# Clustered attention and two MLPs on one core: the order of the attention rewritten as one pipeline over a pair of heads

## The chip, the cores and the metric

One Trainium2 chip, one core of it. The metric is the device time of one execution in microseconds, the median over several runs. The engines are called as the profile calls them: PE (TensorE; PEld is its weight loads), DVE (VectorE), ACT (ScalarE), POOL (GpSimd) and SP (SyncE), whose only work here is to issue DMAs.

## What is computed

Two batches of eight heads, 768 tokens, 64 values a head, everything in 32-bit floats. Each query and key is assigned to the nearest of 16 centroids of its head; a query attends only to the keys of its own cluster. The 1536 rows of 512 values that come out go through two MLPs.

```
q_assign = argmax(q_n . c_n), k_assign = argmax(k_n . c_n)      # 16 clusters a head
scores = scale * q @ k.T, -1e9 where q_assign != k_assign
attn = exp(scores - max(scores)); attn = attn / (sum(attn) + 1e-9)
x = attn @ v                                                     # 1536 x 512
h = max(x @ w1, x @ w2, x @ w3); x = h @ w_out                   # 512 -> 768 -> 512
h = x @ w_in; h = max(0.01 * h, h); out = h @ w_out2             # 512 -> 2048 -> 512
```

## The kernel before

The kernel runs under a manual schedule: each engine executes its instructions in the order in which the program issues them, and waits by semaphores where it needs another engine's result. So the order in which the program is written decides what waits for what.

**Attention.** The 16 heads are 8 pairs. A pair has six units: a unit is one head and 256 of its 768 queries, in two halves of 128. Unit n goes through these steps, named by letters in the table ORDER:

- S0, S1 (`scores`, L608): the scores of a half, four matmuls into one of two score tiles in PSUM (`s`). Two matmuls read the operands q1 and k1, two read q2 and k2, which also hold the one-hot clusters and the mask.
- M0, M1 (`maxima`, L614): the row maximum, on DVE, out of PSUM.
- X0, X1 (`exps`, L620): the exponential, on ACT, from the score tile into one of six buffers `ee` in SBUF, with the row sum.
- R (`inverse`, L628, L629): the reciprocal of the sums, on DVE. Q0, Q1 (`normal`, L634): the division, on POOL.
- T0, T2, T4 (`transposes`, L641): four PE transposes each, into one of three PSUM tiles `t`. E0, E2, E4 (`out_of_psum`, L654 on ACT, L656 on DVE): the copy to `et`; WAYS says which engine, A or D.
- V (`values`, L664): 24 matmuls for two units at once, reading `rv`, into the one tile `o`. Y (`store`, L670): the copy of it on ACT into `acc`.

Beside these run, once a pair, the steps that prepare later pairs. G, C, H, Na, Nb, W, FA, FB find the clusters (PE, ACT, PE, DVE, DVE, POOL, DVE, DVE). O and P turn them into rows `oo`. QH, KH, QL, KL split q and k into high and low parts `qh`, `kh`, `ql`, `kl`. LD and LV load q, k and v of a pair (`rq`, `rk`, `rv`; three buffers of `rv`). D0 and D1 (`operands`, L537) are ten DMAs each on SP's queue, which put these parts together: D0 fills q1, k1 and the upper part of q2 from qh, kh, ql; D1 fills k2 from kl and, from `oo`, the mask rows of q2 and k2, first for the first head of the pair, then for the second.

ORDER has six rows, one for each unit of a pair. An entry `S0/-2` means step S0 of unit n+2 in row n, so scores run two units ahead of the transposes (`T0/0`), and the values of a pair of units end one unit behind (`V/1`). An entry `LV+2` means the load for two pairs later. BEGIN writes out the first three units by hand; ONCE inserts single steps, among them the fetches `f` and the pieces `w` that split the first MLP unit's weights (DVE and ACT); END is the seam to the MLPs.

**MLPs.** Matmuls 128x128 by 128x512 in three products for each block (`three`, L238 to L240), 3 blocks of 512 tokens, weight units 0 to 13. Weights come as raw words and are split on DVE and ACT while PE works (`Weights`).

Of the kernel before, what the change touches and what calls it, by code (L numbers as in the profile page):

```python
# [36 lines left out]
ORDER = (  # L37
# [6 lines left out]
)  # L44

BEGIN = (
# [4 lines left out]
)  # L51
# [3 lines left out]
ONCE = {  # L55
# [10 lines left out]
}  # L66
WAYS = ("ADA", "DAD")
ENGINE = {"QH": "A", "QH@1": "P", "KH": "P", "KL": "P", "KL@0": "D", "W": "P", "W@1": "D"}
WARM = (8, 4)
PACE = 0.16  # L70
FIRST = ("G", "C", "H", "Na", "Nb", "O", "P", "W", "FA", "FB", "QH", "KH", "QL", "LD", "LV")
SPARE = {"O": (2, 0), "O0": (2, 0), "O1": (3, 0)}
HALF = S // 2
# [7 lines left out]
def clustered_attention_mlps(  # L81
# [229 lines left out]
    with ExitStack() as att:  # L311
# [11 lines left out]
        until_transposes = att.enter_context(ExitStack())  # L323
        ep = pool(until_transposes, "ep", 6, side="right")
        until_exps = att.enter_context(ExitStack())
# [185 lines left out]

        def all_onehot_T(p, spare):
            oh = st[p]["oh"][:, D:].rearrange("p (t x) -> p t x", t=NQ // 2)
            ps = spare.bitcast(BF16)[:, 0:HALF]
            for t in range(NQ // 2):
                nc.tensor.transpose(ps[:, t * P : (t + 1) * P], oh[:, t, :], idb)

        def all_penalties(p, spare):
            oo = sm.tile([P, HALF], F32R, tag="oo", name=f"oo{p}", bufs=1)
            st[p]["oo"] = oo  # L520
            nc.scalar.activation(
                oo, spare.bitcast(BF16)[:, 0:HALF], AF.Identity, scale=gain2, bias=base2
            )
# [9 lines left out]
        def operands(p, part, heads=(0, 1), queue=nc.sync):  # L533
# [5 lines left out]
            for j in heads:  # L539
# [12 lines left out]
                else:  # L552
                    q1, q2, k1, k2 = s[j]
                    if part != 2:
                        dma(k2[0:D], s["kl"][r])
                    if part != 1 and p >= 2:
                        for b in range(4):
                            rows = slice((2 * b + j) * C, (2 * b + j + 1) * C)
                            cols = slice(b % 2 * HALF, (b % 2 + 1) * HALF)
                            dma((q2, k2)[b // 2][D : D + C, cols], s["oo"][rows])  # L560
                    elif part != 1:
                        dma(q2[D : D + C], s["oo"][j * C : (j + 1) * C])
                        dma(k2[D : D + C], s["oo"][(2 + j) * C : (3 + j) * C])
# [32 lines left out]
        def scores(n, i, parts=(0, 1)):  # L596
            p, j, g = unit(n)
            q1, q2, k1, k2 = st[p][j]
            if n not in un:
                un[n] = {"e": [], "sum": sums[n % len(sums)]}  # L600
            c0 = g * G + i * P
            if 0 in parts:
                un[n]["s", i], un[n]["spare", i] = bank()
            ps = un[n]["s", i]
            for part in parts:
                a, b, start = ((q1, k1, True), (q2, k2, False))[part]
                for lo, hi in ((0, 512), (512, S)):
                    nc.tensor.matmul(  # L608
                        ps[:, lo:hi], a[:, c0 : c0 + P], b[:, lo:hi], start=start, stop=not start
                    )  # L610
# [36 lines left out]
        def out_of_psum(n, k):  # L647
            p, j, g = unit(n)
            u = un[n]
            if k == 0:  # L650
                u["et"] = done[p, g, j] = etp.tile([P, NQ, G], F32, tag=f"et{j}", name=f"et{n}")
# [29 lines left out]

        def spare(p, op, ahead):

            if p < ahead:
                return scrap((op, p) if p == 0 else p)[:, 256 * p * int(op[1]) :]
            r, i = SPARE[op]
            return un[(p - ahead) * 2 * NG + r]["spare", i]

        def take_apart(op):

            u, c = int(op[1]), int(op[2])
            if op[0] == "f":
                weights.fetch(u, c)
                return
            if (u, c) not in pieces:
                pieces[u, c] = weights.piece(weights.raw.pop((u, c)), u, wa, c)
            next(pieces[u, c], None)

        def do(op, at):
# [25 lines left out]
            elif op == "O":  # L725
                all_onehot_T(at, spare(at, op, 1))
            elif op == "P":
                all_penalties(at, spare(at, "O", 1))
            elif o == "G":
                sims(at, d, spare(at, op, 2))  # L730
            elif op[0] == "N":
                j = int(op[1])
                if op[2] == "a":
                    near_max(at, j, spare(at, f"G{j}", 2))
                else:
                    near_eq(at, j)
            elif op == "W":
# [3 lines left out]
            elif op == "FB":  # L741
                first_eq(at)
            elif o == "O":
                onehot_T(at, d, spare(at, op, 1))
            elif o == "P":
                penalties(at, d, spare(at, f"O{d}", 1))
            elif o == "D":
# [23 lines left out]

        pieces, scraps = {}, {}
        if True:
# [57 lines left out]
            def start(op):  # L831
# [7 lines left out]
                elif op in ("LDq", "LDk"):  # L839
                    load_pair(1, op[2], nc.scalar)  # L840
                elif op in ("LV0", "LV1"):
                    load_pair(int(op[2]), "v", (nc.scalar, nc.sync)[int(op[2])])
                elif op in ("Wq", "Wk"):
# [22 lines left out]
                elif op == "in":  # L866
                    until_scores.close()
                    open_inputs()
                elif op == "ph":
                    until_exps.close()  # L870
# [4 lines left out]
                elif op[0] == "x":  # L875
                    split_x(0, (int(op[1]),))
                else:
                    take_apart(op)

# [12 lines left out]
            for op in BEGIN.split():  # L892
                other(op)
            for n in range(NU):
                c, r = divmod(n, 2 * NG)
                for item in ORDER[r].split():
                    op, sign, by = item.partition("/" if "/" in item else "+")
                    for x in ONCE.get((n, op), "").split():
                        other(x)
                    if sign == "/":  # L900
                        at = n - int(by)
                        if 0 <= at < NU and f"{op}:{at}" not in begun:
                            do(op, at)
                    else:
                        at = c + int(by)
                        first = 2 if op in FIRST else 1
                        if first <= at < NPAIR and f"{op}@{at}" not in begun:
                            do(op, at)

            until_transposes.close()  # L910
            open_hidden()
            for op in END.split():
# [71 lines left out]
```

## Time and profile before

| what | us |
|---|---|
| median of 3 runs | 774.8 (774.32 to 777.26) |
| the profiled execution | 774.25 |
| its span in the trace | 772.3 |
| PE busy in the span | 712.8 (92%) |
| DVE, ACT, POOL busy | 509.3 (66%), 327.6 (42%), 214.8 (28%) |

The span falls in two parts. Up to about 315 us the attention runs, with PE at seven or eight tenths in most slices; from there the MLPs run with PE at nine tenths or more. The busy share of PE counts matmuls from their start to their modelled end, so neighbours overlap; where it matters, the text goes by the distance between starts. In the rows below, `x4` is a count, and a time in square brackets is how long the engine sat idle before the row and for whom.

### The profile page before, as it was taken

How to read it: one execution, taken by the hardware profiler on the slowest of the kernel's cores; microseconds unless marked ns; L12 is line 12 of the kernel's file. 1: busy time of each engine (PE TensorE's matmuls, PEld its weight loads, DVE VectorE, ACT ScalarE, POOL GpSimd, SP SyncE). 2: the span in 40 equal slices, each digit the busy share in tenths (PEclk: the TensorE clock that was granted, in tenths of full speed). 3: DMA queues.
4: the chain of work that ended last, by engine and by line, in shares of the span. 5: the costliest groups of instructions: out<-in, count | busy, mean ns of one | idle time of the engine just before them, and what ended most of it. 6: DMA issues, size and time to landing. Idle time of an engine off the chain costs nothing.

```text
span 772.3 us, 10290 instructions
## 1 busy us (share of the span) xinstructions
PE 712.8 (92%) x3734; PEld 561.1 (73%) x3734; DVE 509.3 (66%) x924; ACT 327.6 (42%) x613; POOL 214.8 (28%) x195
## 2 busy tenths in 40 slices
PE   8797878787878788999999999999999999999998
PEld 5565656565656566788888888888888888888886
DVE  7457667575757556688887829977944983984222
ACT  7354546464555555453332213445543432333220
POOL 1435344443435334011110111122322322232220
PEclk9699999999999999999999999999999999999999
DMA  3765253616262500066455404532641551430012
GB/s 105 190 200 127 69 129 125 160 48 173 79 162 48 147 1 1 27 228 204 155 170 169 163 29 137 179 122 85 211 140 42 189 167 39 154 119 1 27 42 95
DMA packets 29954, 89.96 MB, mean 116 GB/s; under 512 B 4720, under 2 KB 5488, under 8 KB 29904
## 3 DMA queue, kind: packets, MB, share of 16 engines
q1 hardware_dynamic: 29472, 88.14, 37.4%
q10 hardware_dynamic: 432, 1.18, 0.5%
q8 instruction: 29, 0.48, 0.2%
q14 instruction: 21, 0.17, 0.1%
HBM read 68.16 MB, written 3.15 MB: 92 GB/s over the span
## 4 chain that ended last, share of the span: by engine, by line
PE 80%; ACT 6%; POOL 5%; DVE 4%; issue 3%; DMA 1%; POOLq 0%; SPq 0%; ACTq 0%; DVEq 0%
PE h L238 12%; PE h L239 12%; PE h L240 12%; PE o L664 8%; PE y L238 8%; PE y L240 8%; PE y L239 8%; PE t L641 6%; ACT ee L620 5%; PE s L608 5%; POOL ee L634 4%; DVE mx L614 2%; POOL kl L371 1%; DMA rk<-in_kT 1%; PE warm L788 1%
## 5 line engine op out<-in xcount | busy, mean ns | idle before, releaser
L272 POOL TENSOR_TENSOR hl<-a,hh 128x512 fp32r<-128x512 f32 x66 | 91.8, 1391 | 350.6 <-ACT hh L271 350.6
L238 PE MATMUL h<-xh,wh 128*128 128x512 f32 x408 | 159.1, 390 | 0.0
L240 PE MATMUL h<-xh,wl 128*128 128x512 f32 x408 | 158.8, 389 | 0.0
L239 PE MATMUL h<-xl,wh 128*128 128x512 f32 x408 | 158.7, 389 | 0.0
L634 POOL TENSOR_SCALAR ee<-ee,rs 128x768 f32<-128x768 f32 x96 | 95.0, 1001 | 182.7 <-PE t L641 99.7
L641 PE MATMUL t<-idf,ee 128*128 128x128 f32 x576 | 96.3, 292 | 32.6 <-POOL ee L634 32.4
L614 DVE TENSOR_REDUCE mx<-s 128x1 f32<-128x768 f32 x96 | 91.0, 948 | 38.3 <-PE s L608 37.2
L608 PE MATMUL s<-k,q 128*128 128x512 f32 (+3 forms) x384 | 96.5, 376 | 21.2 <-ACT ee L620 20.2
L641 PEld LDWEIGHTS t<-idf,ee 128*128 128x128 f32 x576 | 69.0, 147 | 58.5 <-POOL ee L634 42.8
L620 ACT ACTIVATE ee<-s,mx 128x768 f32<-128x768 f32 x96 | 86.5, 904 | 43.0 <-DVE mx L614 42.7
L238 PE MATMUL y<-hh,wh 128*128 128x512 f32 x264 | 102.7, 389 | 0.0
L239 PE MATMUL y<-hl,wh 128*128 128x512 f32 x264 | 102.7, 389 | 0.0
L240 PE MATMUL y<-hh,wl 128*128 128x512 f32 x264 | 102.7, 389 | 0.0
L271 ACT CAST hh<-a 128x512 fp32r<-128x512 f32 x66 | 41.1, 623 | 125.8 <-DVE a L265 75.0
L238 PEld LDWEIGHTS h<-xh,wh 128*128 128x128 f32 x408 | 76.6, 188 | 16.1 <-issue 0.4
L240 PEld LDWEIGHTS h<-xh,wl 128*128 128x128 f32 x408 | 76.6, 188 | 16.1
L239 PEld LDWEIGHTS h<-xl,wh 128*128 128x128 f32 x408 | 76.6, 188 | 15.7
L608 PEld LDWEIGHTS s<-k,q 80*128 80x128 f32 (+1 forms) x384 | 61.7, 199 | 34.0 <-ACT ee L620 27.1
L263 ACT COPY a<-h 128x512 f32<-128x512 f32 x66 | 38.7, 586 | 95.8 <-PE h L240 94.2
L298 DVE TENSOR_TENSOR acc<-y,acc 128x512 f32<-128x512 f32 x72 | 48.6, 685 | 40.5 <-PE y L240 40.5
L267 DVE SCALAR_TENSOR_TENSOR a<-a,h 128x512 f32<-128x512 f32 x48 | 32.8, 684 | 61.8 <-ACT a L263 61.6
L654 ACT COPY et<-t 128x512 f32<-128x512 f32 x72 | 42.0, 584 | 72.2 <-PE t L641 72.0
(102 smaller groups left out, 866.4 us busy)
## 6 DMA issues: line engine op xcount, KB each, us to landing
raw<-in_w SPq DMA_DIRECT2D x56, 512.0 KB, 3.9
low<-in_w SPq DMA_DIRECT2D x56, 511.5 KB, 3.5
q<-qh SPq DMA_DIRECT2D x28, 192.0 KB, 3.1
k<-kh SPq DMA_DIRECT2D x28, 192.0 KB, 3.7
out_T<-acc SPq DMA_DIRECT2D x12, 256.0 KB, 2.0
rq<-in_qT SPq DMA_DIRECT2D x7, 384.0 KB, 3.7
rk<-in_kT SPq DMA_DIRECT2D x7, 384.0 KB, 5.7
rv<-in_v SPq DMA_DIRECT2D x7, 384.0 KB, 4.3
```

Of the source, the lines that this page charges most:

```text
L238: nc.tensor.matmul(ps, ah, bh, start=(k == 0), stop=False)
L239: nc.tensor.matmul(ps, ah, bl, start=False, stop=False)
L240: nc.tensor.matmul(ps, al, bh, start=False, stop=(k == n - 1))
L272: nc.gpsimd.tensor_tensor(hlo[:, f, :], a, hh[:, f, :].bitcast(F32), op=ALU.subtract)
L298: nc.vector.tensor_tensor(a, ps, a, op=ALU.add)
L608: nc.tensor.matmul(ps[:, lo:hi], a[:, c0 : c0 + P], b[:, lo:hi], start=start, stop=not start)
L614: nc.vector.tensor_reduce(mx, un[n]["s", i], axis=AX.X, op=ALU.max, negate=True)
L620: nc.scalar.activation(e, u.pop(("s", i)), AF.Exp, bias=u.pop(("m", i)), scale=1.0, accum_out=u["sum"][:, i, 0:1],)
L634: nc.gpsimd.tensor_scalar(e, e, un[n]["rs"][:, i : i + 1], 1.0, op0=ALU.mult, op1=ALU.mult)
L641: nc.tensor.transpose(ps[:, kk, i * P : (i + 1) * P], u["e"][i][:, (k + kk) * P : (k + kk + 1) * P], idf,)
L654: nc.scalar.copy(out, ps)
L664: nc.tensor.matmul(un[n]["o"][j * D : (j + 1) * D], v[:, t, j, :], done[p, g, j][:, t, :], start=(t == 0), stop=(t == NQ - 1),)
```

## The change

The table ORDER is replaced by another one, over the same steps, and the program that reads it now runs it from six rows before the first unit to six rows after the last. Three things in it are different throughout.

- Scores of unit n+3 are issued beside the transposes of unit n (S0/-3, S1/-3; in rows 3 and 4 even S0/-4), where before it was n+2. The values follow up to two rows behind the transposes of their units, so that scores may be four units ahead of values or more.
- `ep` has eight buffers of exponentials, not six. The two score tiles, the three tiles `t` and the one tile `o` stay.
- WAYS sends two of the three copies of each unit to ACT and one to DVE; before, odd units had it the other way round.

The steps of the coming pairs have new places. D0 for the next pair stands first in row 0, then LD and LV; D1 stands in row 1, where it was in row 3. V of the last two units of a pair stands in row 1 of the next pair, behind LV in the program; before, it was in row 0, ahead of it. The splitting of the first weights goes by steps `F` and `w` inside the rows, five a pair, in place of the list in ONCE, and starts right after BEGIN. The first two fetches for weight unit 1 (f10, f11) are no longer made during the attention. Since the table now starts six rows early, S0 and S1 of unit 0, which BEGIN writes under other names (SA, SB), are issued a second time.

```diff
 ORDER = (
-    "M1/-1 T0/0 X1/-1 E0/0 S0/-2 R/-1 Q0/-1 O+1 T2/0 Q1/-1 V/1 E2/0 QL+1 M0/-2 P+1 T4/0 E4/0 S1/-2 X0/-2",
-    "M1/-1 T0/0 X1/-1 E0/0 Y/2 S0/-2 R/-1 Q0/-1 KL+1 T2/0 Q1/-1 E2/0 M0/-2 T4/0 E4/0 D0+1 LV+2 S1/-2 X0/-2",
...
+    "R/-1 E2/1 X1/-2 Nb+2 D0+1 Q1/0 Q0/-1 R/-2 T4/1 S0/-3 T0/0 E4/1 S1/-3 E0/0 M0/-3 LD+3 LV+2 X0/-3 "
+    "M1/-3 T2/0 T4/0 X1/-3 Q1/-1",
+    "T0/0 S0/-3 Q0/-1 Y/4 E2/1 QH+2 T2/0 S1/-3 W+2 FA+2 M0/-3 D1+1 F+0 Q1/-1 M1/-3 R/-2 X0/-3 Q0/-2 V/2 "
+    "E2/0 E4/1 X1/-3",
...
-WAYS = ("ADA", "DAD")
+WAYS = ("ADA", "ADA")
...
-        ep = pool(until_transposes, "ep", 6, side="right")
+        ep = pool(until_transposes, "ep", 8, side="right")
...
+        def fetch_pieces():
+
+            while len(fetched) < min(UW // WP, len(taken) + 2):
+                weights.fetch(0, len(fetched))
+                fetched.append(len(fetched))
...
-            for n in range(NU):
+            for n in range(-2 * NG, NU + 2 * NG):
```

On ACT, in the middle of the attention, the copies `et` tell which unit is being transposed and the exponentials `ee` which unit's scores are at hand. Before, where units 19 and 20 are transposed:

```order
L620 ACTIVATE ee20_0_1506,sums0_107<-s40_1457,mx20_0_1491 128x768
L620 ACTIVATE ee20_1_1515,sums0_107<-s41_1501,mx20_1_1508 128x768
L670 COPY acc1_65<-o17_1475 128x256
L654 COPY et19_1517<-t19_2_1531 128x512
L156 ACTIVATE low0_1_656<-low0_1_656 128x512
L620 ACTIVATE ee21_0_1573,sums1_108<-s42_1520,mx21_0_1540 128x768
L620 ACTIVATE ee21_1_1582,sums1_108<-s43_1568,mx21_1_1575 128x768
L654 COPY et20_1584<-t20_0_1577 128x512
```

And of the change, at the same units:

```order
L613 ACTIVATE ee22_0_1631,sums2_109<-s46_1590,mx22_0_1613 128x768
L647 COPY et18_1558<-t18_4_1577 128x512
L613 ACTIVATE ee22_1_1650,sums2_109<-s47_1605,mx22_1_1626 128x768
L647 COPY et19_1647<-t19_0_1585 128x512
L160 CAST wh0_538<-wx0_2_1121 128x512
```

Before, the exponentials of unit 21 stand between the copies of units 19 and 20; now those of unit 22 stand right ahead of the first copy of unit 19, and the copy of v's result (`acc`) has moved elsewhere.

On SP's queue, where the operands of pair 4 are put together (`rv` is a load of v, `kl` and `oo` are the sources of D1). Before:

```order
L537 DMA q1_4_1_1557<-ql4_1489 64x768
L353 DMA rv5_1566<-in_v 128x768
L537 DMA k2_4_0_1551<-kl4_1529 64x768
L537 DMA q2_4_0_1549<-oo4_1493 16x384 x2
L537 DMA k2_4_0_1551<-oo4_1493 16x384 x2
```

And of the change:

```order
L530 DMA q1_4_1_1523<-ql4_1320 64x768
L346 DMA rq6_1562<-in_qT 128x768
L346 DMA rk6_1564<-in_kT 128x768
L346 DMA rv5_1566<-in_v 128x768
L530 DMA k2_4_0_1517<-kl4_1463 64x768
L530 DMA q2_4_0_1515<-oo4_1488 16x384 x2
L530 DMA k2_4_0_1517<-oo4_1488 16x384 x2
```

The queue's order is nearly the same; rq and rk of a later pair have come in ahead of rv5. rv5 takes the buffer of rv2 in both kernels, so it waits for the last matmul that reads rv2, which is in o17.

On PE, what stands between that last matmul of o17 and the first scores of pair 4 (s50) in the change:

```order
L657 MATMUL o17_1634<-et17_1486,rv2_389 64x256
L601 MATMUL s48_1652<-k1_3_1_1155,q1_3_1_1153 128x512
...
L634 MATMUL t19_4_1664<-idf_102,ee19_0_1434 128x128
...
L601 MATMUL s49_1673<-k1_3_1_1155,q1_3_1_1153 128x512
...
L634 MATMUL t20_0_1684<-idf_102,ee20_0_1490 128x128
...
L634 MATMUL t20_2_1696<-idf_102,ee20_0_1490 128x128
...
L634 MATMUL t20_4_1701<-idf_102,ee20_0_1490 128x128
...
L601 MATMUL s50_1706<-k1_4_0_1516,q1_4_0_1514 128x512
...
L601 MATMUL s50_1706<-k2_4_0_1517,q2_4_0_1515 128x512
```

Two scores, four groups of transposes and the first half of s50 stand between the last read of rv2 and the first read of k2_4_0, which is filled by DMAs that stand behind rv5 on SP.

## Rows read from the trace of the kernel before

**Rows 1.** Stretches: heavy pairs, light pair, MLPs, a stretch at low clock.
```profile
core 0: us, PE busy (x) PEld busy (x) DVE busy (x) ACT busy (x) POOL busy (x), PEclk, DMA share, GB/s
74.82:261.94 187.12, 151.38 (x1032) 108.44 (x1034) 124.43 (x215) 98.40 (x202) 80.07 (x76) 0.96 0.43 112
261.94:293.02 31.08, 27.18 (x194) 20.24 (x196) 19.06 (x35) 17.62 (x37) 8.96 (x10) 0.99 0.14 45
320.00:772.30 452.30, 448.55 (x1979) 371.06 (x1978) 305.82 (x536) 158.30 (x275) 91.80 (x66) 1.00 0.37 124
145.93:151.86 5.93, 5.93 (x35) 4.01 (x36) 2.76 (x6) 0.59 (x1) 1.79 (x2) 0.71 0.41 98
```

**Rows 2.** Waits of PE from 74.82 to 261.94: us in total, times, longest.
```profile
PE t L641 <- POOL ee L634: 19.6, 20, 2.3
PE s L608 <- ACT ee L620: 15.9, 20, 1.7
```

**Rows 3.** PE in order of time (start us, us): distances of starts.
```profile
114.68 0.52 PE L483 MATMUL g<-rq,cb 128*32 128x384 f32 x2
...
115.47 0.66 PE L641 MATMUL t<-idf,ee 128*128 128x128 f32 x4
...
118.07 0.97 PE L608 MATMUL s<-k,q 128*128 128x512 f32 x4 [0.35 <-ACT ee L620]
118.88 1.04 PE L641 MATMUL t<-idf,ee 128*128 128x128 f32 x8
119.67 0.95 PE L608 MATMUL s<-k,q 128*128 128x512 f32 x4
...
124.03 2.81 PE L664 MATMUL o<-et,rv 128*64 128x256 f32 x24
126.78 0.66 PE L641 MATMUL t<-idf,ee 128*128 128x128 f32 x4
```

**Rows 4.** A maximum on DVE and a unit's two divisions on POOL.
```profile
119.49 1.97 POOL L634 TENSOR_SCALAR ee<-ee,rs 128x768 f32<-128x768 f32 x2 [6.87 <-PE t L641]
...
120.61 0.94 DVE L614 TENSOR_REDUCE mx<-s 128x1 f32<-128x768 f32 x1
```

**Rows 5.** Two stops of PE, in order of time.
```profile
140.89 0.97 PE L608 MATMUL s<-k,q 128*128 128x512 f32 x4 [1.67 <-ACT ee L620]
...
145.93 0.58 PE L641 MATMUL t<-idf,ee 128*128 128x128 f32 x3 [2.33 <-POOL ee L634]
```

**Rows 6.** SP's queue (start, us of issue) around one load of v.
```profile
142.12 0.89 SPq L353 DMA_DIRECT2D rv<-in_v  x1
...
145.57 1.18 SPq L537 DMA_DIRECT2D q<-oo  x2
146.80 1.22 SPq L537 DMA_DIRECT2D k<-oo  x2
```

**Rows 7.** DMA issues: KB each, median us from issue to landing.
```profile
k<-oo SPq DMA_DIRECT2D x24, 24.0 KB, 1.9
```

**Rows 8.** All DMAs into the operands k1 and k2: landing.
```profile
DMA to landing us min/median/max: 1.8/2.6/5.8
```

**Rows 9.** Start: around the first scores after BEGIN, in order of time.
```profile
33.18 0.88 ACT L620 ACTIVATE ee<-s,mx 128x768 f32<-128x768 f32 x1
33.33 1.14 PEld L608 LDWEIGHTS s<-k,q 128*128 128x128 f32 x4 [1.05 <-ACT oo L529]
...
39.07 0.90 ACT L620 ACTIVATE ee<-s,mx 128x768 f32<-128x768 f32 x1 [0.52 <-DVE mx L614]
...
44.49 0.54 DVE L504 TENSOR_REDUCE m<-near 128x24 f32<-128x384 f32 x1
```

**Rows 10.** Seam to the MLPs: the fourth last and the last value step.
```profile
292.94 2.81 PE L664 MATMUL o<-et,rv 128*64 128x256 f32 x24
...
312.63 2.81 PE L664 MATMUL o<-et,rv 128*64 128x256 f32 x24
```

**Rows 11.** DVE's copies of the transposes in one heavy pair: count, busy us, mean ns.
```profile
L656 DVE COPY et<-t 128x512 f32<-128x512 f32 x9 | 6.1, 678 | 1.4 <-PE t L641 1.4
```

More of the change, by code (lines that the diff above doesn't have):

```diff
@@ L37 @@
 ORDER = (
[6 rows of a table removed]
+    "R/-1 E2/1 X1/-2 Nb+2 D0+1 Q1/0 Q0/-1 R/-2 T4/1 S0/-3 T0/0 E4/1 S1/-3 E0/0 M0/-3 LD+3 LV+2 X0/-3 "
+    "M1/-3 T2/0 T4/0 X1/-3 Q1/-1",
+    "T0/0 S0/-3 Q0/-1 Y/4 E2/1 QH+2 T2/0 S1/-3 W+2 FA+2 M0/-3 D1+1 F+0 Q1/-1 M1/-3 R/-2 X0/-3 Q0/-2 V/2 "
+    "E2/0 E4/1 X1/-3",
+    "S0/-3 E0/1 w+0 Q1/-1 w+0 T4/1 KH+2 M0/-3 S1/-3 E4/1 M1/-3 R/-2 T0/0 QL+2 X0/-3 Y/3",
+    "X1/-2 T2/1 T4/1 S0/-3 V/2 E0/1 Q0/-1 E4/1 S1/-3 FB+2 M0/-3 X0/-3 T0/0 E0/0 Q1/-1 E2/1 T2/0 M1/-3 "
+    "S0/-4 T4/0 E2/0 T0/-1 R/-2",
+    "X1/-2 S1/-3 T2/0 E4/1 G+3 E0/0 Q0/-1 Q1/-1 T4/0 M0/-3 X0/-3 R/-2 M1/-3 S0/-4 E2/0 X1/-3 C+3",
+    "T0/0 S1/-3 E4/1 KL+2 O+2 H+3 Y/4 w+0 M0/-3 Q0/-1 M1/-3 Na+3 T2/0 E0/0 P+2 X0/-3 w+0 w+0 V/2",
 )
 BEGIN = (
[4 rows of a table removed]
+    "Zaq LDq Zal Zak LDk Zaj Zam Gq I2 Gk Zar I2 Naq Nbq Wq FAq FBq Zbq UQ Zbk CQ LV0 I6 Nak "
[3 rows of a table added]
 )
@@ L55 @@
 ONCE = {
[10 rows of a table removed]
+    "M1:3": "KL@1", "X1:3": "D0@1 F", "S1:5": "D1@1", "E0:4": "V:2 Y:2",
+    "T0:46": "in x0 x1", "T0:47": "x2 x3 ph h", "T4:47": "h", "E4:47": "oh h",
 }
-WAYS = ("ADA", "DAD")
+WAYS = ("ADA", "ADA")
 ENGINE = {"QH": "A", "QH@1": "P", "KH": "P", "KL": "P", "KL@0": "D", "W": "P", "W@1": "D"}
@@ L70 @@
 PACE = 0.16
-FIRST = ("G", "C", "H", "Na", "Nb", "O", "P", "W", "FA", "FB", "QH", "KH", "QL", "LD", "LV")
-SPARE = {"O": (2, 0), "O0": (2, 0), "O1": (3, 0)}
 HALF = S // 2
@@ L510, in all_eq, with all_onehot_T, all_penalties @@
             nc.vector.tensor_tensor(e, ps, m.to_broadcast(list(e.shape)), op=ALU.is_equal)
-        def all_onehot_T(p, spare):
+        def all_onehot_T(p):
             oh = st[p]["oh"][:, D:].rearrange("p (t x) -> p t x", t=NQ // 2)
-            ps = spare.bitcast(BF16)[:, 0:HALF]
+            ps = st[p]["up"] = st["spare"].bitcast(BF16)[:, 0:HALF]
             for t in range(NQ // 2):
                 nc.tensor.transpose(ps[:, t * P : (t + 1) * P], oh[:, t, :], idb)
-        def all_penalties(p, spare):
+        def all_penalties(p):
             oo = sm.tile([P, HALF], F32R, tag="oo", name=f"oo{p}", bufs=1)
@@ L521, in all_penalties @@
             nc.scalar.activation(
-                oo, spare.bitcast(BF16)[:, 0:HALF], AF.Identity, scale=gain2, bias=base2
+                oo, st[p].pop("up"), AF.Identity, scale=gain2, bias=base2
             )
@@ L555, in operands @@
                         dma(k2[0:D], s["kl"][r])
-                    if part != 1 and p >= 2:
+                    if part != 1 and p >= 1:
                         for b in range(4):
@@ L602, in scores @@
             if 0 in parts:
-                un[n]["s", i], un[n]["spare", i] = bank()
+                un[n]["s", i], st["spare"] = bank()
             ps = un[n]["s", i]
@@ L649, in out_of_psum @@
             u = un[n]
-            if k == 0:
+            if "et" not in u:
                 u["et"] = done[p, g, j] = etp.tile([P, NQ, G], F32, tag=f"et{j}", name=f"et{n}")
@@ L680, in scrap, with take_apart @@
             return scraps[key]
[L682 to L697, printed above, removed]
+        def fetch_pieces():
+            while len(fetched) < min(UW // WP, len(taken) + 2):
+                weights.fetch(0, len(fetched))
+                fetched.append(len(fetched))
+        def take_apart():
+            if len(taken) < len(fetched):
+                c = fetched[len(taken)]
+                if c not in pieces:
+                    pieces[c] = weights.piece(weights.raw.pop((0, c)), 0, wa, c)
+                if next(pieces[c], None) is None:
+                    taken.append(c)
         def do(op, at):
@@ L725, in do @@
             elif op == "O":
-                all_onehot_T(at, spare(at, op, 1))
+                all_onehot_T(at)
             elif op == "P":
[L728 to L736, printed above, removed]
+                all_penalties(at)
             elif op == "W":
@@ L742, in do @@
                 first_eq(at)
[L743 to L746, printed above, removed]
+            elif op == "F":
+                fetch_pieces()
+            elif op == "w":
+                take_apart()
             elif o == "D":
@@ L770, in do @@
                 raise ValueError(op)
-        pieces, scraps = {}, {}
+        pieces, scraps, fetched, taken = {}, {}, [], []
         if True:
@@ L840, in start @@
                     load_pair(1, op[2], nc.scalar)
-                elif op in ("LV0", "LV1"):
-                    load_pair(int(op[2]), "v", (nc.scalar, nc.sync)[int(op[2])])
+                elif op == "LV0":
+                    load_pair(0, "v", nc.scalar)
+                elif op in ("Gq", "Gk"):
+                    sims(0, "qk".index(op[1]), scrap(op))
+                elif op in ("Naq", "Nak"):
+                    near_max(0, "qk".index(op[2]), scrap("G" + op[2]))
+                elif op in ("Nbq", "Nbk"):
+                    near_eq(0, "qk".index(op[2]))
                 elif op in ("Wq", "Wk"):
@@ L868, in start @@
                     open_inputs()
+                elif op == "oh":
+                    until_transposes.close()
+                    open_hidden()
+                elif op == "F":
+                    fetch_pieces()
                 elif op == "ph":
@@ L877, in start @@
                 else:
-                    take_apart(op)
+                    raise ValueError(op)
             NU = NPAIR * 2 * NG
@@ L893, in clustered_attention_mlps, with ordered @@
                 other(op)
-            for n in range(NU):
+            def ordered(op, at):
+                for x in ONCE.get(f"{op}:{at}", "").split():
+                    other(x)
+                if f"{op}:{at}" not in begun and f"{op}@{at}" not in begun:
+                    do(op, at)
+            for n in range(-2 * NG, NU + 2 * NG):
                 c, r = divmod(n, 2 * NG)
                 for item in ORDER[r].split():
[L897 to L903, printed above, removed]
-                    else:
[L905 to L911, printed above, removed]
+                    if "/" in item:
+                        op, by = item.split("/")
+                        if 0 <= n - int(by) < NU:
+                            ordered(op, n - int(by))
+                    else:
+                        op, by = item.split("+")
+                        if op in "wF" or 1 <= c + int(by) < NPAIR:
+                            ordered(op, c + int(by))
+            assert len(taken) == UW // WP
             for op in END.split():
```

21 rows, old and new, of tables (BEGIN, ONCE, ORDER) are left out of this document.

## The prediction

> **What bounds the kernel now.** I read the busy tenths by slices first, then the stretches, then the waits, and last PE in order of time. In the MLPs PE works 448.6 of 452.3 us at the full clock [rows 1]; nothing in the change touches these matmuls, so the time must come from the attention. There I cut the trace at the value steps of PE, since one pair has three of them. From the values of units 4 and 5 (74.82) to those of units 34 and 35 (261.94) run five "heavy" pairs, which also prepare later ones, at 37.4 us each; then comes one "light" pair without that work at 31.1 [rows 1]. In the heavy pairs no engine is full: PE 30.3 of 37.4, DVE 24.9, ACT 19.7, POOL 16.0 [rows 1]. PE stands still for two things: 19.6 us for POOL's division (transposes) and 15.9 us for ACT's exponential (scores, whose two tiles are still being read) [rows 2]. That is a bound by latency: a unit's scores, maximum, exponential, reciprocal and division follow each other, and PE, in order, meets the transposes of that unit too early.
>
> PE's own need is smaller than its busy time, which counts overlapping tails. By distances of starts [rows 3], a half's scores take 0.80 (118.07 to 118.88), four transposes 0.40 (118.88 to 119.67 for eight), a value step 2.75 (124.03 to 126.78), G 0.79 (114.68 to 115.47). A light pair is 12 x 0.80 + 18 x 0.40 + 3 x 2.75 = 25.1; a heavy one has G and, by my estimate at the rate of the transposes, 0.7 for H and O more: 26.6. So 37.4 - 26.6 = 10.8 us of each heavy pair is waiting, draining and low clock.
>
> **The change, part by part.**
>
> *Scores three ahead.* From the last scores of a unit to its first transposes the work is 0.97 [rows 3] + 0.94 + 0.9 + about 0.35 for the reciprocal + 1.97 [rows 4] = 5.1 us, with 0.9 for an exponential from [rows 9]. In the new table PE has sixteen groups of work between S1 of unit 5 (row 2) and T0 of unit 5 (row 5): V once, scores five times, nine transposes, G: 2.75 + 4.0 + 3.6 + 0.8 = 11.2 us. The wait for POOL, 19.6 us, goes. I walked one pair through the table with the durations above, engine by engine, taking for each step the later of its engine being free and its inputs and its buffer being ready. PE then waits only some 0.4 us in a pair (scores of unit 4, for the exponential just ahead). The two score tiles do not bind: a tile needs 0.97 + 0.94 + 0.9 and small gaps, 3 us, for one of every two halves, so 18 us a pair. DVE, which is next, has 24.9 a pair, less three copies of 0.68 that go to ACT [rows 11]: 22.8. ACT gets them: 19.7 + 1.8 = 21.5. Both stay below PE. The two added buffers `ee` cost nothing: in the walk the oldest is free before its next use.
>
> *LV ahead of V.* This is a new wait. The load of v on SP needs the buffer that the last value step of the previous pair reads, and that step now stands in row 1, after LV in the program. SP waits for it, and behind it are queued D1 for the next pair and the fetches F; the scores of the next pair's first unit (row 3) wait for D1. From the end of the value step: the issue of LV 0.89, then kl 0.5, q<-oo 1.18 and the first of two k<-oo 0.6, the last needed one lands 1.9 after its issue [rows 6, 7], with gaps 5.3 to 5.9 us. Meanwhile PE has two scores, four groups of transposes and half of the next scores: 1.6 + 1.6 + 0.4 = 3.6. PE stops 1.7 to 2.3; I take 2.1, once in each of the five heavy pairs (no load of v is left in the light one). If no DMA is late the bound is 0, if they land as in the worst row, 5.8 [rows 8], it is 6.
>
> *The clock.* After a stop of 1.67 the next scores took the usual 0.97; after one of 2.33 the stretch of 5.93 us had a granted clock of 0.71, so part of it at the lower of its two levels (1.2 and 2.4 GHz) [rows 1, 5], where the same work has 0.3 + 0.8 + 0.5 + 2.75 = 4.4: 1.5 lost. The new stop lies between; I take half, 0.7 (bounds 0 and 1.5).
>
> So a heavy pair is 26.6 + 0.4 + 2.1 + 0.7 = 29.8, five are 149.0 instead of 187.1: **-38.1**. A light pair is 25.1 + 0.4 and 0.5 for draining: 26.0 instead of 31.1: **-5.1**.
>
> *The start.* Both kernels run alike until the second exponential of unit 2 (33.18 [rows 9]). Then the change repeats the scores of unit 0, 1.14 twice at this clock [rows 9], the second after that exponential: to about 35.4. G, its copy and H for pair 2 come before the scores of unit 3: to 38. DVE must do two maxima and compares of 0.54 and two weight pieces first [rows 9], then M, X, M, X: the exponentials of unit 3 end at about 43.5, where before they ended at 40.0. From there the new order needs some 27.7 us (a pair without the stop, and a rest) to the values of units 4 and 5: 71.2 instead of 74.8, **-3.6**. Bounds: 69, if the pieces do not hold DVE, and 78.3, if these units keep the old pace.
>
> *The seam.* From the values of units 40 and 41 to those of 46 and 47 it was 19.7 us [rows 10]. Since values now run later, more is left here: three value steps 8.25, two scores 1.6, thirteen groups of transposes 5.2, six blocks of MLP matmuls at 0.69 (three at 0.23), together 19.2, and about 2.8 of waits, as the division of unit 47 comes behind two casts on ACT and DVE: 22.0, **+2.4** (0 to +5).
>
> *The rest.* The two fetches for weight unit 1 now come at the seam. They are needed only after three blocks of the first chunk, 24 us of matmuls, so I cost them at nothing; without that cover it is one landing, about 4 us. F and w only change place.
>
> Sum: -38.1 - 5.1 - 3.6 + 2.4 = -44.4. The profiled execution took 774.25, 0.5 under the median: 774.25 - 44.4 = 729.9. **Forecast 730**, by itself 722 to 738.
>
> **The rivals.**
>
> *The score tiles keep their wait.* The waits for the exponential stay, 15.9 / 5 = 3.2 a heavy pair [rows 2], since `ps_s` still has two tiles, and only POOL's goes. Then a heavy pair has 32.6, not 29.8, and the light one some 2 more: 730 + 14 + 2 = 746. For it speaks that this wait came up 20 times in five pairs, against it that in the walk ACT reaches the exponentials in time, because the maxima no longer stand behind a late transpose. By the Trainium skill ("Perfetto Trace Analysis", Optimization Strategy) consistent bubbles can mean that there isn't enough PSUM for the next tile; it would come to this rival, and here the second of the two rows of waits agrees with it, the first does not.
>
> *No stop at D1.* If the DMAs land while PE is still on earlier work, because PE is late for other reasons, 5 x (2.1 + 0.7) = 14 go: 716.
>
> *SP's queue becomes the bound (slower).* Same place as the stop above. If D1's DMAs, crowded by the faster loop and the load of v, landed twice as late as the worst row, 11.6 us, PE would stop 0.89 + 0.5 + 1.2 + 0.6 + 11.6 + 0.1 - 3.6 = 11.3 a pair, 9.2 more than I take, and the clock would fall each time: 730 + 5 x 10.0 = 780. It ends slower from a stop of 11 us on. The DMA engines are busy 0.43 of the heavy pairs [rows 1], some 0.54 at the new pace, which speaks against it.
>
> **How the numbers follow.** Chances: forecast 0.52, score tiles 0.22, no stop 0.17, SP's queue 0.03, and 0.06 for something between the old and the new pace, mostly at the start. Range 714 to 750: it takes in the first three and the bounds of the stop (0 to 6) nearly whole. A difference of 0.5% is about what a measurement here can tell from none: faster by more 0.94, within 0.03, slower 0.03.
>
> **What would show it.** Right: distances between every third value step of about 30 in the middle pairs and 26 in the light one, PE's wait for POOL near 0, and one stop of about 2 us of PE in front of the k2 half of the scores once a heavy pair, ended by a DMA from oo, with SP waiting for PE just before a load of v. Wrong: PE's waits for the exponential as before (score tiles), no such DMA wait (716), or DVE without gaps in the heavy pairs. MLPs longer than 452 us would show the fetches missed.

## The result, and the profile after

The changed kernel took 731.5 us (median of 4 runs, 727.82 to 732.7), the kernel before 775.9 (774.32 to 777.26): a ratio of 0.9421, with a 95% interval from 0.938 to 0.9462. The forecast was 730, in a range from 714 to 750. The profiled execution took 730.9, with a span of 729.0. In the experiments below the changed kernel ran a second time, on another chip, with 730.6 and a ratio of 0.9406.

The head of the page of the changed kernel, with the span and each engine's busy time:

```profile
span 729.0 us, 10287 instructions
PE 700.5 (96%) x3730; PEld 559.3 (77%) x3730; DVE 494.2 (68%) x898; ACT 337.5 (46%) x637; POOL 215.8 (30%) x195
```

The sum was made by the starts of four value steps, so here are the stretches between them, with the columns of [rows 1]: five heavy pairs, the light pair, the seam up to the last value step, and the MLPs.

```profile
75.16:220.62 145.46, 136.57 (x1020) 104.68 (x1019) 108.88 (x190) 103.22 (x215) 78.60 (x74) 0.98 0.56 137
220.62:246.10 25.48, 25.43 (x193) 20.22 (x192) 16.43 (x30) 18.52 (x39) 10.69 (x12) 1.00 0.12 43
246.10:269.13 23.03, 20.83 (x152) 14.96 (x151) 9.66 (x18) 12.97 (x27) 6.32 (x6) 1.00 0.01 1
277.00:729.00 452.00, 448.05 (x1977) 370.68 (x1975) 305.32 (x535) 158.11 (x275) 92.03 (x66) 1.00 0.38 123
```

A heavy pair takes 29.1 us (145.46 / 5) instead of 37.4, with almost the same counts of instructions; the light one 25.48 instead of 31.08, and in it PE is busy 25.43. (The two old figures are cut at value steps that are one step late; like steps are set against each other below, under "A mislabelled row".) The MLPs are what they were [rows 1]: from the last value step to the end it is 459.9 us (729.0 - 269.13), before it was 459.7 (772.3 - 312.63). So the gain of 43.3 us of span lies wholly in the attention.

What PE waited for in the five heavy pairs (us in total, times, longest), to be held against the two rows of [rows 2]; PE has no other row there:

```profile
PE s L601 <- DMA k<-oo: 8.8, 5, 2.6
```

POOL's 19.6 and ACT's 15.9 us are gone. In their place there is one new wait, five times, of 1.20, 2.02, 2.58, 1.32 and 1.72 us. The second of them, in the order of PE (start, duration, what it waited for in brackets); the last matmul that reads the old `rv` ends at 106.06:

```profile
105.99 0.97 PE L601 MATMUL s<-k,q 128*128 128x512 f32 x4
106.80 0.60 PE L634 MATMUL t<-idf,ee 128*128 128x128 f32 x4
107.16 0.94 PE L601 MATMUL s<-k,q 128*128 128x512 f32 x4
107.94 1.48 PE L634 MATMUL t<-idf,ee 128*128 128x128 f32 x12
109.17 0.59 PE L601 MATMUL s<-k,q 128*128 128x512 f32 x2
111.77 0.61 PE L601 MATMUL s<-k,q 80*128 80x512 f32 x2 [2.02 <-DMA k<-oo]
112.32 4.50 PE L657 MATMUL o<-et,rv 128*64 128x256 f32 x24
```

And what SP issues at the same time:

```profile
95.51 1.19 SPq L346 DMA_DIRECT2D rk<-in_kT  x1
106.10 0.33 SPq L346 DMA_DIRECT2D rv<-in_v  x1
106.48 0.47 SPq L530 DMA_DIRECT2D k<-kl  x1
107.04 1.68 SPq L530 DMA_DIRECT2D q<-oo  x2
108.77 1.21 SPq L530 DMA_DIRECT2D k<-oo  x2
```

SP issues nothing from 96.70 to 106.10. The load of `rv` stands at the head of its queue and waits for the value step; it goes out 0.04 us after the last read. D1's DMAs follow it one by one, and PE goes on 1.8 us after the last of the two k<-oo is issued (109.98 to 111.77). Meanwhile PE did the two scores, the four groups of transposes and the first half of a score that the prediction had counted, 3.7 us of work.

The clock: behind the stop of 2.02, and likewise behind that of 2.58, the value step took 4.50 us, at a mean granted clock of 0.62; behind the one of 1.32 (as behind 1.20 and 1.72) it took the usual 2.81, at 1.00:

```profile
142.83 0.59 PE L601 MATMUL s<-k,q 80*128 80x512 f32 x2 [2.58 <-DMA k<-oo]
143.34 4.50 PE L657 MATMUL o<-et,rv 128*64 128x256 f32 x24
...
172.73 0.61 PE L601 MATMUL s<-k,q 80*128 80x512 f32 x2 [1.32 <-DMA k<-oo]
173.28 2.81 PE L657 MATMUL o<-et,rv 128*64 128x256 f32 x24
```

### The profile page after: what moved, and what is told of

Read it like the earlier page. It is cut to its first block, busy times and chain, and to the rows that moved or that the text cites. A ratio compares the mean times of both kernels' runs of the same rounds, so it can differ in the third digit from the quotient of the medians.

```text
span 729.0 us, 10287 instructions
## 1 busy us (share of the span) xinstructions
PE 700.5 (96%) x3730; PEld 559.3 (77%) x3730; DVE 494.2 (68%) x898; ACT 337.5 (46%) x637; POOL 215.8 (30%) x195
## 4 chain that ended last, share of the span: by engine, by line
PE 90%; DVE 3%; ACT 2%; DMA 2%; SPq 1%; POOL 1%; issue 1%; ACTq 0%; POOLq 0%; DVEq 0%
PE h L231 13%; PE h L233 13%; PE h L232 13%; PE o L657 10%; PE y L233 8%; PE s L601 8%; PE y L231 8%; PE y L232 8%; PE t L634 7%; DMA k<-oo 2%; SPq L530 1%; ACT ee L613 1%; DVE mx L607 1%; POOL ee L627 1%; PE g L476 1%
## 5 line engine op out<-in xcount | busy, mean ns | idle before, releaser
L601 PE MATMUL s<-k,q 128*128 128x512 f32 (+3 forms) x392 | 99.4, 376 | 14.0 <-DMA k<-oo 8.8
L634 PE MATMUL t<-idf,ee 128*128 128x128 f32 x576 | 81.8, 279 | 8.1 <-POOL ee L627 7.0
L601 PEld LDWEIGHTS s<-k,q 128*128 128x128 f32 (+1 forms) x392 | 63.3, 201 | 29.2 <-ACT ee L613 10.7
L634 PEld LDWEIGHTS t<-idf,ee 128*128 128x128 f32 x576 | 67.5, 143 | 19.4 <-POOL ee L627 8.7
L291 DVE TENSOR_TENSOR acc<-y,acc 128x512 f32<-128x512 f32 x72 | 48.6, 685 | 40.5 <-PE y L233 40.5
L647 ACT COPY et<-t 128x512 f32<-128x512 f32 x96 | 55.0, 592 | 42.1 <-PE t L634 42.0
```

Source lines behind the costliest of these rows:

```text
L291: nc.vector.tensor_tensor(a, ps, a, op=ALU.add)
L601: nc.tensor.matmul(ps[:, lo:hi], a[:, c0 : c0 + P], b[:, lo:hi], start=start, stop=not start)
L634: nc.tensor.transpose(ps[:, kk, i * P : (i + 1) * P], u["e"][i][:, (k + kk) * P : (k + kk + 1) * P], idf,)
L647: nc.scalar.copy(out, ps)
```

## The experiments

Four questions: what the stop at D1 costs; whether the chain through POOL, or PE, now sets the pace; what the small parts (buffers, WAYS) are worth; and what holds up the start. "Changed" means the kernel of the change, "before" the one before. All ratios are to runs of before on the same chip. Where profiles are compared, the changed kernel's own spread counts: its second profile (a0_after) has the value step that was 75.16 at 72.50, and then 147.42, 25.48 and 24.65 for the heavy pairs, the light one and the seam. The 2.7 us at the start come from its first 35 us: the same eleven transposes at about 20 us took 2.61 us in the first profile and 1.42, at a granted clock of 1.00, in the second, and the second exponential of unit 2 ended at 33.6 and 31.0.

**The changed kernel again, beside the next three.**

> The changed kernel again, on the chip of the runs that follow, so that they can be set against it. Expected 731 us, ratio to the kernel before 0.942.

Measured: 730.6 (728.29 to 734.01), ratio 0.9406 (0.9378 to 0.9434).

**LV behind V.** The load of v moves from row 0 to the end of row 1, behind D1 and the value step V.

```
-    "... M0/-3 LD+3 LV+2 X0/-3 "
+    "... M0/-3 LD+3 X0/-3 "
...
-    "E2/0 E4/1 X1/-3",
+    "E2/0 E4/1 X1/-3 LV+2",
```

> The load of v for two pairs later is issued behind the value step that it waits for (end of row 1), so D1 is no longer queued behind that wait. Theory (SP's queue causes PE's one stop a heavy pair): the five stops, 8.8 us in all, and the two stretches at low clock behind the longest, 1.7 us each, go; 731 - 12 = 719, and no wait of the scores for DMA k<-oo in the heavy pairs. Rival (the stop only covers another wait, score tiles or DVE): those waits grow by as much, 728 to 731.

Measured: 716.0 (713.38 to 718.86), ratio 0.9219 (0.9193 to 0.9244): 14.5 us less than the changed kernel beside it, 2.5 more than the 12 expected. The 12 were read from the first profile; in the second, the one beside this run, the five stops are 9.2 us and three value steps behind them ran at the low clock (4.50, 4.50 and 4.39 us), together some 14. Heavy and light pairs of this kernel, columns as above:

```profile
71.09:203.10 132.01, 131.96 (x1020) 103.14 (x1019) 108.46 (x190) 103.23 (x215) 78.62 (x74) 1.00 0.59 147
203.10:228.58 25.48, 25.43 (x193) 20.22 (x192) 16.44 (x30) 18.53 (x39) 10.70 (x12) 1.00 0.13 43
```

PE is busy 131.96 of 132.01 us, at a granted clock of 1.00, and has no wait left in the heavy pairs. On SP the first two k<-oo, those for which PE had stopped, now leave while the value step is still running (it ends at 92.23), some 4 us before PE needs them, and the load of `rv` comes nine us after them:

```profile
91.67 1.22 SPq L530 DMA_DIRECT2D k<-oo  x2
...
94.84 1.22 SPq L530 DMA_DIRECT2D k<-oo  x2
...
100.60 0.33 SPq L346 DMA_DIRECT2D rv<-in_v  x1
```

SP still waits 18.2 us in all for value steps before its loads of v, but nothing that PE needs soon is queued behind them. So the stop and the low clock behind it come from the place of one load in a queue, and the waits for the exponential (the score tiles) do not come back when the stop goes.

**A second pass on POOL, in both kernels.** The division of each unit's second half is followed by a multiplication by one: 48 passes more, about 1 us each [rows 4].

```
             nc.gpsimd.tensor_scalar(e, e, un[n]["rs"][:, i : i + 1], 1.0, ...)
+            if i == 1:
+                nc.gpsimd.tensor_scalar(e, e, 1.0, 1.0, op0=ALU.mult, op1=ALU.mult)
```

In the changed kernel:

> The changed kernel with a second pass of POOL over the second half of each unit (a multiplication by one), 48 passes of about 1.0 us, each between the exponential and the transposes of its unit. Theory (the new lead leaves 6 us of slack between them, and POOL is busy 16 of 29 us a pair, so that 22 still fit): within 5 us of the changed kernel, 731 to 736. Rival (the chain of a unit is still the bound): 48 us more, 779.

In the kernel before:

> The kernel before with the same second pass of POOL. Theory (a unit's chain of exponential, reciprocal, division and transposes bounds it): each pass lengthens the attention by most of its 1.0 us, 30 to 48 us more, 805 to 822. Rival (before, too, PE or the score tiles bound it): under 10 us more, 775 to 785.

Measured: changed 737.8 (736.54 to 739.5), ratio 0.9484 (0.9435 to 0.9534), 6 to 7 us over the kernel without it. Before 807.1 (803.48 to 810.45), ratio 1.0373 (1.0305 to 1.044), 30 us, as the theory had it. For the changed kernel it allowed 5, so the measured cost is a little more. Of some 48 us of work on POOL the old order lets 30 through to the end, the new one 6 or 7. These don't lie in the pairs (heavy 147.75, light 25.44: as without it) but at the two ends, where the chain of one unit still stands free: the value step of the first heavy pair comes at 77.98, and the seam takes 26.59. At the seam PE waits for POOL once for long; the first fence is the changed kernel's seam, the second that with the second pass:

```profile
PE t L634 <- POOL ee L627: 1.8, 2, 1.5
```

```profile
PE t L636 <- POOL ee L629: 2.4, 1, 2.4
```

Most of what the seam lost against the first profile (23.03) is not the wait itself but the clock behind it: the next seven transposes took 1.75 us and the value step 4.70, against 0.98 and 2.81.

**Four transposes of each unit twice, in both kernels.** 48 groups of four more, 0.40 us each [rows 3], 19 us of work for PE.

```
-            for kk in range(2):
+            for kk in (0, 1, 0, 1) if k == 0 else (0, 1):
```

In the changed kernel:

> The changed kernel with the first four transposes of each unit made twice: 48 times 0.40 us, 19 us of PE. Theory (PE is the bound of the new attention): nearly all of it shows, less what falls into the stops at D1 and at the start, 14 to 19 us more, 745 to 750. Rival (DVE or the score tiles are the bound): under 8 us more.

In the kernel before:

> The kernel before with the same second set of transposes. Theory (PE waits 10.8 us of 37.4 in a heavy pair, but the transposes are themselves a link of the chain): less shows than in the changed kernel, 4 to 14 us more, 779 to 790. Rival (PE is the bound before as well): 19 us more, 794.

Measured: changed 743.7 (742.65 to 745.12), ratio 0.956 (0.951 to 0.9609), about 12 us over; a little less than expected. Before 780.5 (778.04 to 782.44), ratio 1.0038 (1.0009 to 1.0067), 3.4 us, within 779 to 790 but just under the 4 us named. In the light pair of the changed kernel all of it shows: 25.48 becomes 28.03, 2.55 for 6 groups, or 0.42 each.

```profile
228.34:256.37 28.03, 27.99 (x217) 22.80 (x216) 16.51 (x30) 18.60 (x39) 10.66 (x12) 1.00 0.08 29
```

In the heavy pairs, with 30 groups or 12 us, only 5 to 7 show. Part of the work falls into the stops at D1, whose row shrinks from 8.8 (9.2 in the second profile) to the row below, and no value step behind them runs at the low clock any more (all five 2.81 us), which gives back 3.4 (5.0):

```profile
PE s L601 <- DMA k<-oo: 6.5, 5, 2.0
```

The two pairs of runs cross over: POOL's time cost 30 us in the old order and 6 or 7 in the new, PE's 3.4 and 12. The bound went from the chain of a unit to PE.

**Seven buffers of exponentials.** Changed kernel, `"ep", 8` made 7.

> The changed kernel with seven buffers of exponentials in place of eight (with six, an exponential would need a buffer whose transposes stand behind it in the program). Theory (the eighth is free long before its use): at most 3 us more, 731 to 734. Rival (the buffers carry the gain): 10 us more or over.

Measured: 740.2 (737.95 to 743.15), ratio 0.9522 (0.9468 to 0.9576), some 9 us more, against at most 3 expected. The light pair takes 28.14 instead of 25.48. PE's waits in the pairs now have ACT at their head, and ACT in turn waits for transposes to free a buffer (all engines, 100 to 215 us):

```profile
ACT ee L613 <- PE t L634: 19.2, 14, 2.6
...
PE s L601 <- ACT ee L613: 6.4, 8, 1.0
...
PE s L601 <- DMA k<-oo: 1.4, 3, 0.8
```

The loop needs the eighth buffer; without it PE's scores wait for the exponential as they did in the kernel before, and part of that lies where the stop at D1 would have been.

**The old WAYS.** Changed kernel, with the copies of odd units as before, two on DVE and one on ACT.

```
-WAYS = ("ADA", "ADA")
+WAYS = ("ADA", "DAD")
```

> The changed kernel with the old shares of copies (two of three on DVE in odd units). DVE then has 2.0 us a pair more and ACT 1.8 less. Theory (PE bounds, DVE has about 6 us of 29 free): within 5 us, 731 to 736. Rival (DVE is nearly the bound): 2.0 a pair, 15 us more, 746.

Measured: 740.4 (738.6 to 744.43), ratio 0.9531 (0.9484 to 0.9579), again some 9 us more, between the theory (within 5) and the rival (15). DVE is busy 114.58 us of the 154.28 that the heavy pairs then take, far from full; but the maxima stand behind copies that wait for transposes, the exponentials behind the maxima, and PE's scores behind the exponentials (100 to 215 us):

```profile
ACT ee L613 <- DVE mx L607: 17.3, 16, 2.5
...
PE s L601 <- DMA k<-oo: 8.1, 4, 2.5
...
PE s L601 <- ACT ee L613: 4.5, 5, 1.3
```

In the changed kernel the first of these rows is 10.2 us over the same window, and the third is not there.

**Both small parts alone.** Kernel before, with WAYS ADA, ADA and eight buffers.

```
-WAYS = ("ADA", "DAD")
+WAYS = ("ADA", "ADA")
...
-        ep = pool(until_transposes, "ep", 6, side="right")
+        ep = pool(until_transposes, "ep", 8, side="right")
```

> The kernel before with the two small parts of the change alone: eight buffers of exponentials and two of three copies on ACT in every unit. Theory (all of the gain is in the order): 770 to 778. Rival (DVE's copies held the chain before): 10 us less or more, under 766.

Measured: 783.4 (780.34 to 789.56), ratio 1.0088 (1.0055 to 1.0122): 6 us slower than before, where 770 to 778 was expected. The two waits of [rows 2] are both still there (PE, 74.8 to 262 us):

```profile
PE t L641 <- POOL ee L634: 21.3, 21, 2.8
PE s L608 <- ACT ee L620: 12.6, 25, 0.9
```

So these two parts bring nothing to the old order, and the whole gain needs the new table; why they cost 6 us there, no run shows. Given the new table, the eighth buffer and the new WAYS are each worth 9 us.

**The start.** BEGIN computes the scores of unit 0, and the table's first rows compute them again, as the prediction said (they aren't in the list `begun`). First this repetition is taken away:

```
-            begun += ["V:1", "Y:1"]
+            begun += ["V:1", "Y:1", "S0:0", "S1:0"]
```

> The second issue of S0 and S1 of unit 0 is left out. Theory (they lie on the path at the start, 3.1 us of PE at low clock, and G, H and the scores of unit 3 wait behind them): 2 to 3 us less than the changed kernel, 728 to 729. Rival (DVE, which waits there for the low words of the weights and takes two pieces, sets the start): no difference, 731.

Measured: 730.0 (726.54 to 731.86), ratio 0.9386 (0.9356 to 0.9417): no difference from 730.6, against 2 to 3 us expected. The value step stands at 72.23 (72.50 in the changed kernel beside it), and counted from the end of the second exponential of unit 2 it is 41.3 us (41.5). The trace shows why, on ACT and PE, in the kernel without the repetition:

```profile
42.08 0.84 ACT L353 ACTIVATE qh<-rq 128x768 fp32r<-128x768 f32 x1 [4.56 <-DMA k<-kh]
```

```profile
43.86 1.65 PE L601 MATMUL s<-k,q 128*128 128x512 f32 x4 [3.39 <-ACT ee L613]
```

and with it, on ACT:

```profile
41.84 0.84 ACT L353 ACTIVATE qh<-rq 128x768 fp32r<-128x768 f32 x1 [1.27 <-DMA q<-qh]
```

QH of pair 2 writes the buffer `qh` that D0's DMAs of pair 1 still read. It starts at 42 in both, ACT's next exponential stands behind it, and PE's scores behind that. The time that PE won became a wait of ACT. So the time is the rival's, but these rows show another cause for it than DVE.

Both edits, LV behind V and no repetition:

> Both edits together (load of v behind the value step, no second scores of unit 0). If the two are separate in time they add: 731 - 12 - 2.5 = 716. If both only move a wait: 725 or more.

Measured: 714.6 (713.65 to 717.58), ratio 0.9204 (0.918 to 0.9227). That is the gain of LV alone; the second edit adds nothing that can be told from the spread.

Then D0 of pair 1 ahead of the load LD of pair 3 on SP, on top of both:

```
-    "M1:3": "KL@1", "X1:3": "D0@1 F", ...
+    "M0:3": "D0@1", "M1:3": "KL@1", "X1:3": "F", ...
```

> Both edits of the run before (load of v behind its value step, no second scores of unit 0), and D0 of pair 1 on SP's queue ahead of the loads of q and k for pair 3, of which the second waits for KL of pair 1. Theory (at the start the exponentials of unit 4 stand on ACT behind QH of pair 2, which waits for D0's DMAs to have read qh of pair 1, 4.0 us without the second scores): this wait goes, the values of units 4 and 5 start some 4 us earlier than 73.2, and the time is 714.6 - 4 = 711, ratio 0.915. Rival (the low clock and the stream of loads at the start hold these units anyway): 713 to 716, ratio 0.919 to 0.922.

Measured: 715.2 (713.52 to 719.65), ratio 0.9181 (0.9138 to 0.9225). By its median this is the rival's 713 to 716; the interval of the ratio holds the theory's 0.915 as well. The long wait of ACT is gone, since QH starts at 40.76 with no wait, but the value step still comes at 73.58 (73.17 without this edit). These two executions had parted before the place of the edit, though: the eleven transposes at about 20 us took 2.61 us here and 1.42 without the edit, at granted clocks of 0.50 and 1.00, and the second exponential of unit 2 ended at 34.3 and 31.8. From there to the value step it is 39.3 us against 41.3. So half of the 4 us shows in the trace, and none of it in the times. The intervals of the three kernels with LV moved overlap; all are about 8% under the kernel before and 2% under the changed one, and none of the three can be told from the others.

What holds up the start beyond this is open. What the rows show is that much of it runs at the low clock and that DVE is busy for most of its second part. From 30 to 50 us, before, changed, and the last kernel:

```profile
30.00:50.00 20.00, 17.98 (x112) 13.12 (x113) 10.77 (x19) 9.49 (x20) 8.27 (x9) 0.83 0.83 247
```

```profile
30.00:50.00 20.00, 16.98 (x67) 12.28 (x68) 11.63 (x19) 8.68 (x17) 7.65 (x8) 0.57 0.75 199
...
43.10:59.15 16.05, 13.84 (x81) 10.94 (x79) 13.30 (x23) 10.21 (x22) 8.56 (x9) 0.85 0.70 160
```

```profile
30.00:50.00 20.00, 14.51 (x63) 10.52 (x64) 13.20 (x24) 9.88 (x20) 9.37 (x9) 0.66 0.85 206
```

Up to 50 us PE's matmuls ran at a granted clock of 0.57 in the changed kernel, 0.83 before; from 43.1 to 59.15 DVE works 13.30 of 16.05 us. Between the two, the second profile of the changed kernel speaks against the clock: its same stretch, from the last exponential of unit 3 to the first value step (40.48 to 56.50), ran at 0.73, with 15.28 us of PE instead of 13.84, and took 16.0 us like the first, with DVE at 13.30 in both. By these two executions PE's clock did not set the length of this stretch. That DVE did is not shown, since no run gives it more or less work here.

## Why the prediction was right

The sum, term by term, by the starts of value steps as the prediction took them:

| term | predicted | measured (second profile) |
|---|---|---|
| start, value step at 74.82 before | 71.2 (69 to 78.3) | 75.16 (72.50) |
| five heavy pairs | 149.0 | 145.46 (147.42) |
| light pair | 26.0 | 25.48 (25.48) |
| seam | 22.0 (19.7 to 24.7) | 23.03 (24.65) |
| last value step to the end | unchanged, 459.7 | 459.9 (460.0) |

That the total came out within 1.2 us is in part luck: in the first profile the start is 4.0 over its term and the seam 1.0, and the pairs are 4.1 under theirs.

**Scores three ahead: right.** The wait for POOL is gone, as the walk had it, and that for the exponential with it, though the two score tiles are the same. The two passes on POOL bear the mechanism out: a longer division costs 30 us in the old order and next to nothing in the pairs of the new one. But no run moves the scores alone, without the other new places in the table, so that it is the lead that does it, and not these, is argued from the walk and not shown. In the kernel with LV moved a heavy pair is PE's own work, 26.4 us (132.01 / 5) where the prediction's estimate was 26.6, and PE waits 0.0, not 0.4. The rival of the score tiles fell. By the Trainium skill ("Perfetto Trace Analysis", Optimization Strategy) a gap that repeats can mean too little SBUF or PSUM for the next tile. As to PSUM the trace disagrees: 15.9 us of score waits [rows 2] went with no PSUM tile added. As to SBUF it agrees in the new order alone (one buffer less, 9 us more), not in the old one, where two more, together with the new WAYS, brought nothing.

**LV ahead of V: right, in its place, size and cause.** Predicted were 5.3 to 5.9 us from the end of the value step to the DMA's landing, and 3.6 of work for PE; in the stop shown it is 5.7 (106.06 to 111.77) and 3.7. Two parts of this sum were off and cancel: the issue of LV took 0.33 us, not 0.89, and PE needs both k<-oo, not the first alone (each fills 384 columns of k2, and the first matmul reads 512); it goes on 2.4 us after the issue of the second began. The mean stop is 1.8 us (8.8 / 5), predicted 2.1. Without it 14.5 us went; the prediction's rival "no stop" said 14. The rival of a stop of 11 us didn't come, though the DMA engines were busy 0.56 of the time, as estimated (0.54). The Trainium skill ("DMA: Bandwidth & Descriptors", Rules for kernel authors) advises to issue a DMA early and wait late; here the measurement goes the other way for one load, since its buffer wasn't free: issued earlier it held up the queue, issued later it cost nothing.

**The clock: right in the sum, not in each stop.** The prediction took half of a loss of 1.5 for every stop, since their length lay between a stop that lost nothing and one that did, 3.5 in five pairs. Two of five stops lost 1.7 each (4.50 - 2.81), 3.4 together, and three lost nothing; in the second profile three lost 5.0 together. That the sum fits is partly luck, as the length of a stop alone does not tell what it loses (see the last part).

**The start: mis-sized.** This is the largest miss beside the pairs, 4.0 us in the first profile and 1.3 in the second, within its bounds. The exponentials of unit 3 ended at 43.1 in the first profile, as predicted (43.5), and at 40.5 in the second. But from there to the value step it took 32.0 us in both (to 75.16 and 72.50), not 27.7. That step carried the pace of the middle into a stretch in which, up to 59.15, DVE is busy 13.30 of 16.05 us and PE waits for the exponentials. So the second profile is nearer to the term only because its first 35 us were faster. The last exponential of unit 3 on ACT, first and second profile:

```profile
42.23 0.89 ACT L613 ACTIVATE ee<-s,mx 128x768 f32<-128x768 f32 x1
```

```profile
39.59 0.89 ACT L613 ACTIVATE ee<-s,mx 128x768 f32<-128x768 f32 x1
```

The repetition of the scores of unit 0, which the prediction charged with twice 1.14 us, cost nothing in the end, for the reason shown above.

**A mislabelled row.** The prediction names the value step at 74.82 as that of units 4 and 5. Counted over all 24 value steps of the trace of before it is that of units 6 and 7; that of units 4 and 5 is at 61.75, and the other marks are likewise one step late (units 34 and 35 at 247.29, 40 and 41 at 282.71). The total is not touched, as the sum runs from the start to the last value step, which is at 312.63 under both counts. The split is: between like steps the start became 13.4 us longer (61.75 to 75.16), which fits the table's running scores further ahead of the first values, though no run measured that apart; the heavy pairs lost 40.1 (185.5 to 145.5), the light one 9.9 (35.4 to 25.5) and the seam 6.9 (29.9 to 23.0), together -43.5. So the new order does cost something at the start, which the prediction's count hid, and gains about half of it back at the seam, which the prediction had down as a loss of 2.4.

**The small parts: a gap in the working.** The prediction held DVE and ACT to stay below PE and the buffers to be free in time. That held, with WAYS and `ep` as they are in the change. It gave no price to being without them; by the runs it is 9 us each. The share of DVE (24.9 of 37.4 [rows 1]) does not show this; the place of the maxima behind the copies in its order does.

## What to carry to other kernels

When an engine waits though none is full, look for the order in which in-order engines meet the steps of one unit; running the first step further ahead took away 35 us of waits here without a tile more in PSUM, though not without another buffer in SBUF. Test which engine sets the pace by doubling a cheap step on each: the cost of the doubled step, not the busy share, tells it. A load whose buffer is not yet free holds up all that is queued behind it on its issuing engine, so put it behind what the bounding engine needs next (14.5 us here for one entry of a table).

## What was not expected of the hardware

After short stops of PE the clock fell in some cases only, and the length of the stop alone does not tell in which. In the first profile of the changed kernel it fell after 2.02 and 2.58 us, and not after 1.20, 1.32 and 1.72. But in the kernel without the repetition it fell after a stop of 1.47 us (value step 4.50 us, granted clock 0.61) and not after one of 2.02 (2.81 us, 1.00), and with the old WAYS after 1.69 and not after 2.54:

```profile
82.78 0.58 PE L601 MATMUL s<-k,q 80*128 80x512 f32 x2 [1.69 <-DMA k<-oo]
83.29 4.44 PE L657 MATMUL o<-et,rv 128*64 128x256 f32 x24
...
146.73 0.59 PE L601 MATMUL s<-k,q 80*128 80x512 f32 x2 [2.54 <-DMA k<-oo]
147.24 2.81 PE L657 MATMUL o<-et,rv 128*64 128x256 f32 x24
```

Nor is it the same in each execution of one kernel: at the seam, after the same stop of 1.50 us, the next seven transposes took 0.98 us in the first profile of the changed kernel and 1.74 in the second, and the value step behind them 2.81 and 3.68.

```profile
261.39 0.98 PE L634 MATMUL t<-idf,ee 128*128 128x128 f32 x7 [1.50 <-POOL ee L627]
```

```profile
260.69 1.74 PE L634 MATMUL t<-idf,ee 128*128 128x128 f32 x7 [1.50 <-POOL ee L627]
```

So the seam was 1.6 us longer in the second (24.65 against 23.03), and differences of this size between single profiles say nothing about an edit.
